# Four single rows in attention, low weight bits by GpSimd, the first feed-forward tiles turned by VectorE and DMA, in a new order

## The chip, the cores and the metric

One core of a Trainium2 chip. Times are microseconds (us) of that core. The kernel before took 346.61 us (median of 3 runs, 345.60 to 346.94).

## What is computed

Chunked attention with memory keys, and a feed-forward layer with SoLU and a normalization, all in float32:

```python
B, H, S, D = 4, 8, 768, 64            # chunk 32, left 16, right 8, 8 memory keys
for c in range(S // 32):               # each chunk of 32 queries sees 64 keys
    k_full, v_full = concat(mem, context of c)
    a = softmax(q_c @ k_full.T / 8)
    x[:, :, chunk c] = a @ v_full
x = x.transpose(0, 2, 1, 3).reshape(3072, 512)
h = x @ w_in                           # 512 x 1024
solu = h * softmax(h)
ln = (solu - mean) / sqrt(var + 1e-6) * g_ln
out = ln @ w_out                       # 1024 x 512
```

The two large products are made from rounded parts: each operand is split into a high part and a low rest, and three products (high x high, high x low, low x high) are summed in PSUM. The weights come as float64 and are put together from the two 32-bit words of each number.

## The kernel before

The 3072 tokens are 24 row tiles of 128. Attention works by items: rows 0 and 1 are an item each (`SINGLES = 2`), the other 22 rows go in 11 pairs. The feed-forward layer works row by row. `ORDER` (L31) is a list of steps that is read once from front to back (L600); a step issues its instructions, so the list sets the order of every engine's queue and of the queue of transfers on SyncE. There is no planner at run time: an engine takes its own instructions in this order and waits where an operand or a buffer isn't there yet.

The steps, with their engines:

- **Loads** (SyncE): `Lq`, `Lk`, `Lv` an item's queries, keys and values (L224); `D` 1 MB of weight words (L255; 0 to 3 are `w_in`, 4 to 7 `w_out`).
- **Weights**: `A` (ScalarE, L259) makes a float32 from the high word, `B` (VectorE, L267) shifts it left by 3, `I` (VectorE, L271) inserts the three top bits of the low word, `H` (L277) rounds to the high part, `L` (L285) makes the low rest. Weight block 0 goes in two cuts.
- **Attention**: `S` scores on TensorE (L343), `M` row maximum, `Bm` difference from it, `Z` sum with its reciprocal (VectorE, L366 to L414), `X` exponentials (ScalarE), then the probabilities are turned: items 0 to 3 by TensorE (`PT`, L332) and a copy `PC`; the others by VectorE in 32x32 blocks (`Pt`, L300) and four transfers of 128 KB (`Pw`, L309) that put the blocks in their place. `V` values on TensorE (L421), `N` division by the sum (VectorE, L446). The result x is turned likewise (`XT` for items 0 to 3, `Xt` and `Xw` for the others) and split (`XH`, `XL`).
- **Feed-forward**: `Gt.c.half` (L500) is three 128x512 matmuls of row t; eight of them make a row of h, in a two-bank PSUM buffer ("two", of which there are 3, shared with scores, values and turned tiles of pairs). `Hm`, `He`, `Hu` are maximum, exponential, product; `C` centers, `Sq` squares, `Dn` the inverse deviation. Then u is turned: rows 0 to 3 by TensorE (`UT`), the others by VectorE and transfers (`Ut`, `Uw`). `UH`, `UL` split it (L485, L492), and `Ot.f` (L567) is three matmuls with `w_out`, eight to a row. `Os`, `St` scale and store.
- `Wu5` (L201) is five matmuls of a zero tile, ten instructions, without use for the result.

Turning by TensorE and turning by VectorE with transfers leave the columns of a tile in different orders. The columns of `w_in` are sorted on the host for the second way; a row that is turned by TensorE reads `w_in` through a rearranged view instead:

```python
        if f"UT{t}" in todo:
            w = [m.rearrange("p (f d n) -> p f n d", d=4, n=SQ) for m in w]
```

Of the kernel before, what the change touches and what calls it, by code (L numbers as in the profile page):

```python
# [13 lines left out]
U32 = mybir.dt.uint32  # L14
AF = mybir.ActivationFunctionType
# [3 lines left out]
P = 128  # L19
# [3 lines left out]
SLOTS, HALVES, RAWS, ROUNDED = 7, 6, 4, 8  # L23
SINGLES = 2
AHEAD = 6
SPLIT = {0: 2}
# [9 lines left out]
Lk3 G1.0.1 H2.0@S L2.0@V G0.2.0 G1.1.0 N2 A4.0 B4.0 I4.0 A6.0 B6.0 L2.1@G G0.2.1 G0.3.0 G0.3.1 Hm0  # L36
G1.1.1 I6.0 XT2 XH2@S XL2@V He0 Lg H4.0@S H4.1@S L4.1@G G1.2.0 G1.2.1 G1.3.0 Hu0 G1.3.1 Hm1 He1 S3
M3 Bm3 G3.0.0 G3.0.1 G3.1.0 G3.1.1 D5 D7 G3.2.0 G2.0.0 G3.2.1 Hu1 G3.3.0 G3.3.1 A5.0 B5.0 X3 PT3
C0@S I5.0 G2.0.1 G2.1.0 C1@G A7.0 Lv3 PC3@S V3 G2.1.1 G2.2.0 G2.2.1 L4.0@G Hm3 He3 Z3 Lv5 Hu3 C3@S
UT3 UH3@S N3 XT3 B7.0 XH3@S I7.0 G2.3.0 G2.3.1 UL3@V O3.0 Lk4 H5.0@S Lq4 S4 XL3@V G4.0.0 G4.0.1 O3.1  # L40
G4.1.0 G4.1.1 H6.0@S Hm2 He2 Lq5 M4 Bm4 UT0 Lv4 Sq3 G4.2.0 Hu2 Lk6 X4 Pt4 H5.1@S Lk5 S5 G4.2.1 UH0@S
UL0@V O0.0 M5 Bm5 G5.0.0 L5.1@V L5.0@G O3.2 Lq7 X5 G5.0.1 UT1 UH1@S O0.1 Pw4 Pt5 G5.1.0 Pr4 H6.1@S
Sq0 H7.0@S Dn3@G L6.0@G O0.2 Dn0@G UL1@V G5.1.1 O0.3 G5.2.0 Z4 L7.0@G V4 N4 Xt4 G4.3.0 O3.3 G4.3.1
Hm4 Lq6 S6 Pw5 O0.4 He4 Lk7 Xw4 O3.4 G5.2.1 H7.1@S L6.1@G O0.5 G5.3.0 M6 Bm6 S7 Hu4 O0.6 O3.5 L7.1@V
O0.7 Os0 Pr5 V5 O3.6 C2@G Xr4 XH4@G XL4@G O1.0 M7 Bm7 X7 Lk8 G5.3.1 Z5 N5 X6 O3.7 Lv7 G7.0.0 G6.0.0
Lq8 Xt5 G7.0.1 G6.0.1 St0 Xw5 G7.1.0 O1.1 Os3 G7.1.1 G6.1.0 G7.2.0 Z6 Sq1 G6.1.1 G7.2.1 Lv6 Pt6 O1.2
G7.3.0 Hm5 He5 Hu5 C5@G Ut5 Pw6 UT2 O1.3 G6.2.0 Xr5 XH5@G O1.4 G7.3.1 UH2@S UL2@V O2.0 Hm7 O1.5 He7
# [43 lines left out]
def chunked_attention_then_solu_kernel(  # L91
# [132 lines left out]
    def load(name, src):  # L224
        def step(i):
# [463 lines left out]
```

## Time and profile before

| | |
|---|---|
| median of 3 runs | 346.61 us |
| the profiled execution | 345.05 us |
| its span (first to last instruction) | 343.3 us |
| mean granted TensorE clock | 0.985 |
| TensorE busy | 324.0 us, 94% of the span |
| VectorE busy | 223.3 us, 65% |
| GpSimd busy | 139.7 us, 41% |
| ScalarE busy | 130.2 us, 38% |
| moved by DMA | 62.38 MB, mean 182 GB/s |

The span is the profiled execution without 1.75 us that lie around it. PE is TensorE, DVE VectorE, ACT ScalarE, POOL GpSimd, SP SyncE. L513 is the line of the hidden layer's matmuls, L573 that of the second product, L353 scores, L437 values, L339 turning on TensorE, L204 the matmuls of zeros. Matmuls overlap, so the time of one is read from a run of them (start to start), not from the mean duration of one. "Issue" is time in which an engine waited for nothing that the profile shows.

### The profile page before, as it was taken

To read this page: it belongs to the slowest core of one execution; us is meant where nothing else is said; L and a number is where in the kernel's file an instruction comes from. 1 tells how busy PE (TensorE), PEld (TensorE's weight loads), DVE (VectorE), ACT (ScalarE), POOL (GpSimd) and SP (SyncE) were. 2 spreads that over 40 slices of the span, in tenths; PEclk is the share of its full clock that TensorE was granted. 3 is DMA by queue.
4 is the path that set the end of the run, shared out by engine and by line. 5 is a ranking of instruction groups with operands and counts; after the bars stand their busy time and mean duration, and the time that the engine had idled before them with its cause. 6 is when DMAs were issued, how large, how long until landed. Compare 5 with 4: busy or idle time off the path is not lost.

```text
span 343.3 us, 9936 instructions
## 1 busy us (share of the span) xinstructions
PE 324.0 (94%) x4324; PEld 262.4 (76%) x4324; DVE 223.3 (65%) x286; ACT 130.2 (38%) x189; POOL 139.7 (41%) x173
## 2 busy tenths in 40 slices
PE   1769999999889999999999999999999999999995
PEld 1657777887678888878888888888888888888784
DVE  1699998987993898866985764737467563046200
ACT  3257364743322243403432315422345175033421
POOL 0228052416216375455525702521176645525250
PEclk9969999999989999999999999999999999999999
DMA  7999933645839276775838686824342505144421
GB/s 292 418 423 414 413 146 109 228 138 164 313 86 329 65 185 153 216 225 151 321 76 251 164 272 138 277 67 113 105 123 64 122 2 122 61 126 133 110 94 61
DMA packets 32299, 62.38 MB, mean 182 GB/s; under 512 B 3712, under 2 KB 23168, under 8 KB 29824
## 3 DMA queue, kind: packets, MB, share of 16 engines
q1 hardware_dynamic: 28800, 55.46, 51.5%
q10 hardware_dynamic: 3456, 6.29, 5.0%
q8 instruction: 34, 0.56, 0.6%
q14 instruction: 9, 0.07, 0.1%
HBM read 35.52 MB, written 6.29 MB: 122 GB/s over the span
## 4 chain that ended last, share of the span: by engine, by line
PE 94%; issue 2%; DMA 2%; DVE 1%; ACT 0%; SPq 0%
PE two L513 40%; PE one L573 39%; PE two L353 6%; PE two L437 5%; PE two L339 2%; DMA k<-in_kw 2%; PE two L204 1%; PE one L339 1%; DVE half L454 0%; DVE half L387 0%; DVE per_head L376 0%; ACT half L581 0%; ACT half L400 0%; SPq L233 0%; SPq L257 0%
## 5 line engine op out<-in xcount | busy, mean ns | idle before, releaser
L513 PE MATMUL two<-w_in_h,fr 128*128 128x512 f32 x384 | 141.3, 401 | 0.0
L573 PE MATMUL one<-w_out_h,fr 128*128 128x512 f32 x384 | 137.9, 396 | 0.0
L513 PEld LDWEIGHTS two<-w_in_h,fr 128*128 128x128 f32 x384 | 72.3, 188 | 18.1
L573 PEld LDWEIGHTS one<-w_out_h,fr 128*128 128x128 f32 x384 | 72.6, 189 | 16.2 <-ACT half L581 0.3
L513 PE MATMUL two<-w_in_l,fr 128*128 128x512 f32 x192 | 76.3, 397 | 0.0
L573 PE MATMUL one<-w_out_l,fr 128*128 128x512 f32 x192 | 75.3, 392 | 0.0
L522 DVE TENSOR_REDUCE per_row<-two 128x1 f32<-128x1024 f32 x24 | 29.1, 1213 | 28.7 <-PE two L513 28.7
L581 ACT ACTIVATE half<-one,per_row 128x512 f32<-128x512 f32 x24 | 16.5, 687 | 81.5 <-PE one L573 73.9
L513 PEld LDWEIGHTS two<-w_in_l,fr 128*128 128x128 f32 x192 | 36.1, 188 | 8.1
L573 PEld LDWEIGHTS one<-w_out_l,fr 128*128 128x128 f32 x192 | 36.3, 189 | 7.2
L220 POOL TENSOR_TENSOR fr<-raw,fr 128x1024 fp32r<-128x1024 f32 x13 | 31.4, 2417 | 16.9 <-ACT fr L215 16.2
L527 ACT ACTIVATE raw<-two,per_row 128x1024 f32<-128x1024 f32 x15 | 16.8, 1118 | 35.1 <-DVE per_row L522 31.0
L353 PE MATMUL two<-k,q 64*32 64x64 f32 x1536 | 20.3, 236 | 10.0 <-DMA k<-in_kw 7.6
L353 PEld LDWEIGHTS two<-k,q 64*32 64x32 f32 x1536 | 17.4, 110 | 14.6 <-DMA q<-in_qT 7.6
L537 DVE CUSTOM_DVE_ANT_0 raw<-two,raw 128x1024 f32<-128x1024 f32 x15 | 18.3, 1218 | 10.9 <-ACT raw L527 9.5
L220 POOL TENSOR_TENSOR fr<-slot,fr 128x1024 fp32r<-128x1024 f32 x9 | 21.6, 2405 | 7.7 <-ACT fr L215 3.6
L217 POOL TENSOR_SCALAR fr<-slot 128x1024 fp32r<-128x1024 f32 x10 | 10.5, 1054 | 34.1 <-PE one L573 22.2
L562 POOL TENSOR_SCALAR per_row<-per_row,per_row 128x1 f32<-128x1 f32 x24 | 7.0, 292 | 39.7 <-ACT raw L554 29.9
L554 ACT ACTIVATE raw<-raw 128x1024 f32<-128x1024 f32 x15 | 15.7, 1049 | 9.0 <-DVE slot L305 9.0
L376 DVE TENSOR_REDUCE per_head<-two 128x16 f32<-128x1024 f32 (+1 forms) x13 | 14.8, 1140 | 5.0 <-PE two L353 4.7
L305 DVE STREAM_TRANSPOSE slot<-raw 128x1024 f32<-128x1024 f32 x12 | 14.8, 1237 | 4.1 <-ACT raw L547 2.6
L549 POOL TENSOR_SCALAR raw<-raw,per_row 128x1024 f32<-128x1024 f32 x6 | 6.8, 1126 | 26.2 <-DVE per_row L540 26.2
(92 smaller groups left out, 375.8 us busy)
## 6 DMA issues: line engine op xcount, KB each, us to landing
v<-in_vw SPq DMA_DIRECT2D x11, 1024.0 KB, 5.8
k<-in_kw SPq DMA_DIRECT2D x11, 672.0 KB, 7.5
slot<-raw SPq DMA_DIRECT2D x48, 128.0 KB, 2.8
out<-half ACTq DMA_DIRECT2D x24, 256.0 KB, 3.2
q<-in_qT SPq DMA_DIRECT2D x11, 512.0 KB, 4.6
raw<-slot SPq DMA_DIRECT2D x44, 128.0 KB, 2.6
raw<-in_w_in SPq DMA_DIRECT2D x4, 1024.0 KB, 9.0
raw<-in_w_out SPq DMA_DIRECT2D x4, 1024.0 KB, 9.1
```

The costliest lines, as they stand in the source:

```text
L220: (nc.gpsimd if on == "G" else nc.vector).tensor_tensor(out, a, b, ALU.subtract)
L305: nc.vector.transpose(t, src.rearrange("p (m d n) -> p d m n", d=4, n=SQ))
L353: nc.tensor.matmul(s[32 * j:32 * j + 32, r, t, g], q[rows, o + t, g, 32 * j:32 * j + 32], k[rows, o + t, g, START[j]:START[j] + KEYS], sta ...
L376: nc.vector.tensor_reduce(nmax, s, axis=AX.X, op=ALU.max, negate=True)
L437: nc.tensor.matmul(x[32 * j:32 * j + 32, r, t, g], pT[rows, t, g, j], vv[rows, o + t, g, j], start=True, stop=True,)
L513: nc.tensor.matmul(h[:, half], x[a], w[b], start=c == 0 and i == 0, stop=c == NC_ - 1 and i == 2,)
L522: nc.vector.tensor_reduce(take("per_row", ("hm", t), 1), flat(get("h", t)), axis=AX.X, op=ALU.max, negate=True)
L527: nc.scalar.activation(take("slot", ("u", t), 2), flat(get("h", t)), AF.Exp, bias=get("hm", t), scale=1.0, accum_out=take("per_row", ("esu ...
L537: nc.vector.tensor_tensor_reduce(u, flat(get("h", t)), u, 1.0, 0.0, ALU.mult, ALU.add, accum_out=usum)
L554: nc.scalar.activation(u, u, AF.Square, accum_out=take("per_row", ("var", t), 1))
L573: nc.tensor.matmul(get("o", t), u[a], w[b][:, f], start=f == 0 and i == 0, stop=f == NF - 1 and i == 2)
L581: nc.scalar.mul(take("half", ("osb", t), 1), get("o", t), get("rstd", t))
```

## The change

- `SINGLES = 4`: rows 0 to 3 are items of their own; 10 pairs follow.
- Step `B` is gone. A new step `T` makes the three low bits: GpSimd reads the top byte of the low word as uint8 (every eighth byte), and computes (byte - 15.5) / 32, which is rounded to an integer as it is written; `I` now shifts and inserts in one instruction.
- No `UT` is left: rows 0 to 3 of u go by `Ut` and `Uw` like the others, and their `G` steps read `w_in` straight. `XT` and `PT` stay for items 0 to 4 (rows 0 to 5, as before), and `N` of these items writes pairs of columns, with `vw` sorted to match on the host.
- The reciprocal is a step of its own, `Zr`: for 10 of 14 items on GpSimd, as a power of -1.
- In rows 0 to 3, `G` is two of the three products, and `K` is the third (high x low), so that it can come later. `G`, `K` and `O` steps come in any order of c and f; the first one to run starts the sum.
- Transfers of turned tiles may be issued by ScalarE (`@S`, 11 of them) instead of SyncE (`@Y`).
- Small pools: 7 instead of 6 "half" buffers, fewer of the smallest.
- The list is new from end to end: `Wu24`, `Wu9` and `Wu1` in place of two `Wu5`, and another order of loads.

```diff
-SLOTS, HALVES, RAWS, ROUNDED = 7, 6, 4, 8
-SINGLES = 2
+SLOTS, HALVES, RAWS, ROUNDED = 7, 7, 4, 8
+SINGLES, AHEAD, AHEAD_X = 4, 6, 6
+SPLIT, SPLIT_ROWS = {0: 2}, 4
 ORDER = """
-D0 CT A0.0 B0.0 A0.1 Lq0 B0.1 I0.0 H0.0@S Lk0 S0 M0 Lq2 Lk2 Bm0 Lk1 Lq1 X0 I0.1 H0.1@S L0.0@G Wu5 Z0
-L0.1@G S2 M2 D3 A3.0 Lv0 D1 PT0 Lv1 D2 Lv2 S1 M1 Bm2 Bm1 X1 PT1 PC0@S B3.0 I3.0 V0 H3.0@G L3.0@G
-H3.1@S Wu5 D4 Z1 D6 A1.0 PC1@S X2 N0 XT0 V1 B1.0 I1.0 H1.0@G L1.0@G PT2 N1 XT1 XH0@S H1.1@S Lq3
-XL0@V G0.0.0 G0.0.1 G0.1.0 A2.0 PC2@S V2 B2.0 XH1@S I2.0 H2.1@S L1.1@G XL1@V G1.0.0 L3.1@G G0.1.1 Z2
...
+Lq1 CT Wu24 D0 T0.0@G A0.1 A0.0 T0.1@G Lk1 Lk3 S1 D3 I0.0 H0.0@G Lq0 T3.0@G I0.1 M1 Bm1 X1 Z1 PT1
+H0.1@G Lq2 Lq3 A3.0 I3.0 H3.1@S H3.0@G S3 Lk2 M3 Bm3 X3 S2 M2 Bm2 Wu9 L0.0@G Zr1@G L0.1@V Lk0 S0 D2
+T2.0@G Z3 A2.0 M0 Bm0 X2 Z2 PT2 PC2@S Lv2 I2.0 D1 T1.0@G PC1@S Zr2@G X0 Z0 V2 PT0 Lv0 A1.0 PT3 PC0@S
+V0 I1.0 H1.0@S Zr0@V N0 Lv1 V1 N1 PC3@S L1.0@V Wu1 H2.1@S XT0 XH0@S XL0@V H1.1@S XT1 Lk4 XH1@S
+K0.1.0 N2 Lv3 V3 H2.0@S L3.0@G D7 K0.0.0 A7.0 G0.0.0 Lq4 L3.1@G G0.2.0 K0.3.0 XL1@V G1.2.1 G0.1.1
...
-    def w_first(i, x):
-        a = cut(get("a", i).bitcast(U32), i, x)
-        nc.vector.tensor_scalar(a, a, 3, None, ALU.logical_shift_left)
+    def low_byte(i, x):
+        w = get("raw", i).bitcast(U8).rearrange("p (n b) -> p n b", b=8)
+        n = w.shape[1] // SPLIT.get(i, 1)
+        return w[:, x * n:(x + 1) * n, 3]
+    def w_bits(i, x, on):
+        t = words(i, x, 0)
+        byte = low_byte(i, x)
+        if on == "S":
+            nc.scalar.activation(t, byte, AF.Identity, bias=down, scale=1.0 / 32)
+        else:
+            nc.gpsimd.tensor_scalar(t, byte, -15.5, 1.0 / 32, ALU.add, ALU.mult)
     def w_insert(i, x):
         a = cut(get("a", i).bitcast(U32), i, x)
-        low = cut(words(i, 0), i, x)
-        nc.vector.scalar_tensor_tensor(a, low, 29, a, ALU.logical_shift_right, ALU.bitwise_or)
+        nc.vector.scalar_tensor_tensor(a, a, 3, words(i, x, 0), ALU.logical_shift_left, ALU.bitwise_or)
...
     def row_sum(i):
...
-        nc.vector.tensor_scalar(s, s, 1e-9, None, ALU.add)
-        nc.vector.reciprocal(s, s)
+    def inverse(i, on):
+        s = get("rinv", i)[:, 0:2 * items[i][1] * NP_]
+        if on == "G":
+            nc.gpsimd.tensor_scalar(s, s, 1e-9, 1.0, ALU.add, ALU.mult)
+            nc.gpsimd.tensor_tensor(s, s, minus[:, 0:s.shape[1]], ALU.pow)
+        else:
+            nc.vector.tensor_scalar(s, s, 1e-9, None, ALU.add)
+            nc.vector.reciprocal(s, s)
...
     def norm(i):
         if f"XT{i}" in todo:
-            x = x.rearrange("p (n m r a) -> p r n a m", m=SQ, r=2, a=2)
+            x = x.rearrange("p (n m r a) -> p r n m a", m=SQ, r=2, a=2)
             for r in range(2):
                 nc.vector.tensor_tensor(
-                    x[:, r], xp[:, r].rearrange("p n (a m) -> p n a m", a=2),
-                    rinv[:, r].unsqueeze(3).broadcast_to([P, n * NP_, 2, SQ]), ALU.mult,
+                    x[:, r], xp[:, r].rearrange("p n (m a) -> p n m a", a=2),
+                    rinv[:, r].unsqueeze(3).broadcast_to([P, n * NP_, SQ, 2]), ALU.mult,
...
+    HH, HL, LH = ("xh", "h"), ("xh", "l"), ("xl", "h")
+    def hidden(products):
+        def step(t, c, half):
+            mine = products if t < SPLIT_ROWS else (HH, HL, LH)
+            for x, w in mine:
...
+                nc.tensor.matmul(h[:, half], xx, ww, start=n == 1, stop=n == 3 * NC_)
...
-                nc.sync.dma_start(t[:, e * q:e * q + e], src[SQ * q:SQ * q + SQ])
+                (nc.scalar if on == "S" else nc.sync).dma_start(
+                    t[:, e * q:e * q + e], src[SQ * q:SQ * q + SQ]
+                )
```

## Rows read from the trace of the kernel before

**Rows 1.** Page of the profile: its first line, and part 1, busy time by engine

```profile
span 343.3 us, 9936 instructions
...
PE 324.0 (94%) x4324; PEld 262.4 (76%) x4324; DVE 223.3 (65%) x286; ACT 130.2 (38%) x189; POOL 139.7 (41%) x173
```

**Rows 2.** Waits of TensorE: engine, line, waited-for, us in total, times, longest

```profile
PE two L353 <- DMA k<-in_kw: 7.6, 1, 7.6
...
PE two L353 <- issue: 2.3, 1, 2.3
PE two L437 <- issue: 2.2, 1, 2.2
```

**Rows 3.** Chain that ended last, in order of time: start, us, what; hidden-layer matmuls

```profile
53.13 1.63 PE two L513 x6
...
140.31 5.44 PE two L513 x24
```

**Rows 4.** Five-microsecond windows, columns: us, PE, PEld, DVE, ACT, POOL, PEclk, DMA share, GB/s

```profile
20.00:25.00 5.00, 4.43 (x85) 3.77 (x86) 4.78 (x9) 4.10 (x6) 1.91 (x2) 0.62 1.01 419
25.00:30.00 5.00, 4.79 (x86) 3.55 (x85) 4.81 (x6) 3.65 (x5) 4.10 (x4) 1.00 1.01 416
...
50.00:55.00 5.00, 5.00 (x56) 3.52 (x55) 4.12 (x5) 2.50 (x3) 3.32 (x3) 1.00 0.00 0
```

**Rows 5.** The same chain: one row tile turned on TensorE, and what follows

```profile
67.93 0.87 PE two L339 x8
68.80 0.70 PE two L513 x3
```

**Rows 6.** The same chain: scores of a pair of row tiles, and what follows

```profile
62.87 1.41 PE two L353 x91
64.28 1.58 PE two L513 x6
```

**Rows 7.** The same chain: the gap inside the values of item 5, and the last piece

```profile
93.15 2.23 issue
95.39 1.07 PE two L437 x54
96.45 2.73 PE one L573 x6
...
339.67 0.69 ACT half L581
```

**Rows 8.** Timeline of the start: start, us, engine, line, operation

```profile
8.72 2.50 PE L204 MATMUL two<-z 128*128 128x128 f32 x10
...
24.50 1.23 DVE L274 SCALAR_TENSOR_TENSOR slot<-raw,slot 128x1024 uint32<-128x1024 uint32 x1
...
27.48 0.52 PE L513 MATMUL two<-w_in_h,fr 128*128 128x512 f32 x1
...
28.39 2.17 DVE L274 SCALAR_TENSOR_TENSOR slot<-raw,slot 128x1024 uint32<-128x1024 uint32 x1
```

**Rows 9.** Groups by line and form: busy us, mean ns, idle before

```profile
L269 DVE TENSOR_SCALAR slot<-slot 128x1024 uint32<-128x1024 uint32 x5 | 3.6, 725 | 0.0
...
L376 DVE TENSOR_REDUCE per_head<-two 128x8 f32<-128x512 f32 x2 | 1.4, 692 | 3.0 <-PE two L353 3.0
...
L387 DVE TENSOR_TENSOR half<-two,per_head 128x512 f32<-128x512 f32 x2 | 1.4, 686 | 0.0
...
L454 DVE TENSOR_TENSOR half<-two,per_head 128x256 f32<-128x256 f32 x4 | 2.2, 648 | 0.2 <-PE two L437 0.2
...
L217 POOL TENSOR_SCALAR fr<-slot 128x1024 fp32r<-128x1024 f32 x10 | 10.5, 1054 | 34.1 <-PE one L573 22.2 <-DMA slot<-raw 10.5 <-DMA slot<-slot 1.3
...
L563 POOL TENSOR_TENSOR per_row<-per_row,mhalf 128x1 f32<-128x1 f32 x24 | 13.3, 553 | 2.0
```

**Rows 10.** The same groups: a transpose on VectorE, and a weight rest on VectorE

```profile
L305 DVE STREAM_TRANSPOSE slot<-raw 128x1024 f32<-128x1024 f32 x12 | 14.8, 1237 | 4.1 <-ACT raw L547 2.6 <-POOL raw L549 1.3
...
L220 DVE TENSOR_TENSOR w_in_l<-slot,w_in_h 128x512 fp32r<-128x512 f32 x1 | 0.6, 627 | 0.0
```

More of the change, by code (lines that the diff above doesn't have):

```diff
@@ L87 @@
+St20 O23.5 O23.6 Dn23@G O23.1 O23.2 Os23 St23
 """
@@ L377, in row_max @@
         used("s", i)
-    todo = set(ORDER.split())
+    todo = set(ORDER.replace("@", " ").split())
     def below_max(i):
@@ L398, in exps @@
     def exps(i):
-        a = get("p", i)
-        nc.scalar.activation(a, a, AF.Exp, scale=scale)
+        if f"Bm{i}" in todo:
+            a = get("p", i)
+            nc.scalar.activation(a, a, AF.Exp, scale=scale)
+            return
+        n = items[i][1] * NP_
+        nmax = get("nmax", i)[:, 0:2 * n]
+        nc.scalar.mul(nmax, nmax, scale)
+        a = take(home(i), ("p", i), 2).rearrange("p (n r k) -> p r n k", r=2, k=KEYS)
+        for r in range(2):
+            for h in range(n):
+                nc.scalar.activation(
+                    a[:, r, h], by_head(i)[:, r, h], AF.Exp, bias=nmax[:, r * n + h:r * n + h + 1], scale=scale
+                )
+        used("s", i)
+        used("nmax", i)
     def row_sum(i):
@@ L468, in source, with target @@
         return (name + "t", i), get(name + "t", i).rearrange("p (q m n) -> p m q n", q=4, n=SQ)
-    def target(name, i, uses):
+    def target(name, i):
         if name[0] == "u":
-            return by_block(take("fr", (name, i), uses))
+            return by_block(take("fr", (name, i), NF))
         first, n = items[i]
-        buf = shared("fr", (name, first // 2), uses)
+        u = first // 2
+        each = [2 if t < SPLIT_ROWS and name == "xh" else 1 for t in (2 * u, 2 * u + 1)]
+        buf = shared("fr", (name, u), 2 * NC_ * sum(each))
         o = first % 2 * HALF
@@ L498, in low @@
         return step
[L500 to L519 removed]
+    HH, HL, LH = ("xh", "h"), ("xh", "l"), ("xl", "h")
+    def hidden(products):
+        def step(t, c, half):
+            u, odd = divmod(t, 2)
+            mine = products if t < SPLIT_ROWS else (HH, HL, LH)
+            h = shared("two", ("h", t), 2)
+            for x, w in mine:
+                xx = get(x, u).rearrange("p (t c n) -> p t c n", t=2, n=P)[:, odd, c]
+                ww = (w_in_h if w == "h" else w_in_l)[:, c, half * HALF:(half + 1) * HALF]
+                if f"UT{t}" in todo:
+                    ww = ww.rearrange("p (f d n) -> p f n d", d=4, n=SQ)
+                n = done[t, half] = done.get((t, half), 0) + 1
+                nc.tensor.matmul(h[:, half], xx, ww, start=n == 1, stop=n == 3 * NC_)
+            for x in sorted({x for x, _ in mine}):
+                used(x, u)
+        return step
     def h_max(t):
@@ L567, in project @@
     def project(t, f):
-        if f == 0:
-            take("one", ("o", t), 1)
+        o = shared("one", ("o", t), 1)
         u = [get(n, t)[:, f * P:(f + 1) * P] for n in ("uh", "ul")]
         w = (w_out_h, w_out_l)
-        for i, (a, b) in enumerate(((0, 0), (0, 1), (1, 0))):
-            nc.tensor.matmul(
-                get("o", t), u[a], w[b][:, f], start=f == 0 and i == 0, stop=f == NF - 1 and i == 2
-            )
-        if f == NF - 1:
-            used("uh", t)
-            used("ul", t)
+        for a, b in ((0, 0), (0, 1), (1, 0)):
+            n = done[t] = done.get(t, 0) + 1
+            nc.tensor.matmul(o, u[a], w[b][:, f], start=n == 1, stop=n == 3 * NF)
+        used("uh", t)
+        used("ul", t)
     def scale_out(t):
```

208 lines of the change are left out of this document (92 added, 116 removed).

## The prediction

> **What bounds the kernel now.** I read the page first: TensorE is busy for 324.0 of 343.3 us, the next engine, VectorE, for 223.3 [rows 1]. Then the waits of TensorE: what costs more than a fraction of a microsecond is the wait for the first keys (7.6), one for the probabilities of row 1, and two of about 2.2 us, called issue, which no buffer or operand explains [rows 2]. The third view is the chain that ended last. From the first hidden-layer matmul, which starts at 27.48 us [rows 8], to the last scaling at 339.67 [rows 7] it is TensorE's own work nearly throughout. So there are two prices: what comes off TensorE's work in these 312 us comes off the time, one for one, as long as the other engines keep up; and ahead of 27.48 us a chain of transfers, VectorE and ScalarE decides.
>
> The reader should look at two things within the 312 us. A hidden-layer step has three matmuls. In the stretch at 140.31, 24 of them take 5.44 us: 0.2267 each. But at 53.13 six take 1.63: 0.272 each [rows 3]. The granted clock is 1.00 there, and the transfers are at rest from 50 to 55 us [rows 4], so it is neither. What sets this stretch apart is the row: it belongs to rows 0 to 3, which read `w_in` through the rearranged view of `UT`.
>
> **Part by part, on TensorE.**
> Turning of u for rows 0 to 3: four times eight transposes, 0.87 us each, and the step behind takes 0.70 instead of 0.68 [rows 5]. It goes to VectorE and transfers: 4 x 0.89 = -3.6 us.
> Straight reading of `w_in`: four rows of 24 matmuls, 96 x (0.272 - 0.2267) = -4.4 us. The Trainium skill (TensorE: Matmul & The Clock Gate, Wait — 56ns, not 53.3ns?) has the distance of matmuls at full clock set by their columns alone. By that this term would be nothing and the sum 4.4 us higher; here the two kinds differ by 20% at the same clock, and the measurement decides.
> Scores and values: a pair takes 1.41 us and about 0.22 more in the step behind it (1.58 for six matmuls that take 1.36) [rows 6]. Before, values of one pair that is now single rows are computed behind 27.48, after it those of row 3 alone: half of 1.41, -0.7. The transposes of x and of the probabilities are as many as before, and so are the matmuls: splitting a step into `G` and `K` adds none.
> The gap at 93: values of item 5 stop halfway for 2.23 us; the two steps that then run as six matmuls take 2.73 instead of 1.36, and the second half of the values takes 1.07 where half of 1.41 would do [rows 7]. That is 2.23 + 1.37 + 0.36, about -4.0 if it doesn't come back. It came while scores and values of pairs ran close together: nine matmuls, 2 us, lie between scores 7 and values 5 in the old list. In the new one no two steps of scores or values of pairs have fewer than 15 between them, 3.4 us. I therefore take it as gone; the other bound is that one such gap comes elsewhere, 0, and two would be +4.
>
> **The start.** The first keys come behind the same bytes as before (a 1 MB block and one row's queries), so at 7.6 us [rows 2]. `Wu24` is 48 instructions. The first ten of before took 2.50 us [rows 8], a turned tile takes 0.109 per instruction when the engine is fast [rows 5]: between 5.2 and 11.7 us. TensorE began to work at 7.6, and all ten of those, from 8.72 to 11.2, were slow; so I take 3.6 us at that rate, 15 at 0.24 and 33 at 0.14, over at about 9.3; scores of row 1 end at 10. Then VectorE has an unbroken list up to x of rows 0 and 1: four maxima, four differences and four sums at 0.69 [rows 9], three inserts at 1.23 [rows 8], one rest of 0.63 [rows 10], two divisions of at most 2 x 0.65 [rows 9], 0.6 of small ones: 8.3 + 3.7 + 0.6 + 2.6 + 0.6 = 15.8. With `L1.0` (0.63) and half a microsecond of waits the first `K` runs at 26.9, -0.6 against 27.48. The bounds: 4 earlier (the zeros end before the keys come, the divisions are shorter with paired columns) and 4 later (zeros at the slow rate to the end, or an issue gap as the one of 2.3 us in the scores before [rows 2]).
> The nine shifts `B` (0.73 for a whole block [rows 9]) go. On the path that is three of them, which the list above no longer has; the others are nothing, as VectorE has free time later. Nine `T` come on GpSimd; the nearest row is a one-operand pass of 1.05 us [rows 9]. `T1.0` is the last on the path and runs beside `A1.0`: nothing, and about 1 us if it comes behind it. The reading of every eighth byte may raise it, at most to the two-fold, in the same place.
> **Clock.** TensorE has waits ahead of the first step in either list, and the granted clock fell to 0.62 between 20 and 25 us [rows 4]. Before, ten useless matmuls ran in that stretch and the clock was full from 25 on; now two do (`Wu1`). Half a clock over the first 2 to 3 us: +1.0 (0 to +3).
>
> **What the others must now do.** Four times a transpose of 1.24 on VectorE [rows 10] against the subtractions `UL` of these rows that move from VectorE to GpSimd: about even, and the shifts and reciprocals that leave it make it lighter. The four transfers of each of the four rows, and their issue on SyncE, lie under the hidden steps of rows 1 to 4, some 25 us of TensorE's work from the end of row 0 to its first use; what is queued behind `Uw0` on SyncE is the queries and values of item 6, which are wanted only behind the values of item 5. 44 issues on ScalarE's queue lie in its free 62%. New waits in a list of which every place has changed: I take +1.5, with 0 below (there is hardly one now) and +6 above (three or four rows of h that wait for a buffer held by VectorE).
>
> **Sum.** -3.6 - 4.4 - 0.7 - 4.0 - 0.6 + 1.0 + 1.5 = -10.8. The profiled execution took 345.05 (1.75 around its span), which gives 334.2. The median of the runs shown is 1.56 above it: 335.8, say 336.
>
> **The rivals.**
> *The gap comes back.* Nothing in the trace names its cause, only its neighbourhood; instructions of scores and values are still issued by the hundred, and transfers move 419 GB/s ahead of the first step [rows 4]. Then 340.
> *VectorE and GpSimd in each other's way.* An insert beside GpSimd's subtractions took 2.17 us, one of the same form alone 1.23 [rows 8]. GpSimd gets the nine `T`, the `UL` of four rows and the reciprocals, most of it in the first 60 us, where VectorE is the second busiest. Eight such collisions behind the start and on the path would add 8 x 0.9 = 7: 343. Against it: TensorE has a stock of steps that can run, and hardly waited for VectorE so far. The Trainium skill (GPSIMD Engine Reference, Engine selection) would keep such elementwise passes on VectorE, and says (Key points) that the two share interfaces to the memory; the two inserts agree.
> *Slower: the power on GpSimd.* A power of one column takes 0.55 us [rows 9]. If its price went by columns, a reciprocal of 8 would take 4.4 and one of 16 8.8. `Zr1`, `Zr2` and `Zr4` stand in GpSimd's queue ahead of the rests `L3`, `L1`, `L2` and of `L4`, and the hidden steps of rows 0 and 1 need those: 2 x 4.4 ahead of `L3.0` and 8.8 ahead of item 4's division, 17.6 in all, as TensorE then runs dry. 345 - 12.3 + 17.6, and the median's 1.6, is 352. It turns at 12.3 us for 32 columns, 0.38 us a column. Against it: one column in 0.55 is little more than the other one-column operations of GpSimd in the profile.
> *The slow matmuls aren't due to the view.* Then 4.4 stay, 340 (what the rule named above would give). The stretch with idle transfers speaks against it.
>
> **How the numbers follow.** Forecast as summed 0.50; gap again 0.20; collisions 0.13; the power 0.06; matmuls not faster 0.04; 0.07 for a wait that I don't see. The range takes in the gap, the slow matmuls and most of the collisions: up to 343; below, a start 4 us earlier and no new waits: 336 - 5 = 331. 0.5% is 1.7 us, about what a measurement of this kernel tells from no change. Faster than 344.9: 0.50 + 0.20 + 0.04 + most of the 0.13 and some of the rest, 0.88. Slower than 348.3: the power and a part of the unseen, 0.08. Between: 0.04.
>
> **What would show it.** Right: six hidden matmuls in 1.36 from the first row on; no transposes of u on TensorE; the first hidden matmul at 25 to 28 us; GpSimd's power at 1 us or less; no issue gap behind 30 us; TensorE's work unbroken to the end. Wrong: a wait of TensorE for VectorE or GpSimd of several microseconds in the first 60 us, or rows 0 to 3 still at 0.272.

## The result, and the profile after

Over 20 runs each, the changed kernel takes 349.12 us (median) and the kernel before 346.10: the ratio is 1.0073, with a 95% interval of 1.0051 to 1.0096. The change makes the kernel slower by 0.7%; 336.0 had been forecast. The profiled execution of the changed kernel took 346.47 us, 1.42 more than the one of before, and the readings of this section are of that one. It is the second fastest of the 20 (345.68 to 355.00), 2.65 below their median, so it shows 1.4 of the 3.0 us between the medians; what the rest may be comes with the traces of later runs. Every ratio here leaves out disturbed executions, and the profiled ones of two later runs (zeros narrow, four loads later) were such, with longer spans (351.0 and 355.4 us), so that from these two only single waits ahead of 80 us are read.

The head of the page, the busy time of each engine, and from the part on queues the one by which instructions come:

```profile
span 344.7 us, 10028 instructions
...
PE 323.9 (94%) x4340; PEld 265.2 (77%) x4340; DVE 212.7 (62%) x271; ACT 136.1 (39%) x196; POOL 169.5 (49%) x199
...
q8 instruction: 34, 0.56, 0.7%
```

TensorE is as busy as before [rows 1], with fewer transposes, more useless matmuls, and more of its time at half clock (mean granted clock 0.979 instead of 0.985). What it waited for (engine, line, waited-for, us in total, times, longest):

```profile
PE two L359 <- issue: 4.0, 1, 4.0
PE two L463 <- issue: 3.9, 2, 2.3
PE one L598 <- ACT half L603: 3.9, 2, 3.0
PE one L345 <- ACT half L407: 2.6, 2, 2.3
```

The wait for the first keys [rows 2] is gone from the list, because 48 useless matmuls now fill it. Instead of 4.5 us there are 7.9 called issue, in three places, and 3.9 for ScalarE's scaling of the second product. The three places are in TensorE's timeline of the start (start, us, engine, line, operation, in brackets the idle time before):

```profile
1.04 7.97 PE L212 MATMUL two<-z 128*128 128x128 f32 x48 [1.04 <-DVE z L199]
8.94 0.86 PE L359 MATMUL two<-k,q 64*32 64x64 f32 x64
...
12.62 1.65 PE L359 MATMUL two<-k,q 64*32 64x64 f32 x105
18.22 0.65 PE L359 MATMUL two<-k,q 64*32 64x64 f32 x23 [3.96 <-issue]
18.80 4.21 PE L212 MATMUL two<-z 128*128 128x128 f32 x18
...
27.81 0.99 PE L463 MATMUL two<-v,half 64*32 64x64 f32 x74 [0.46 <-ACT half L223]
31.09 0.77 PE L463 MATMUL two<-v,half 64*32 64x64 f32 x54 [2.30 <-issue]
...
33.41 0.49 PE L541 MATMUL two<-w_in_l,fr 128*128 128x512 f32 x1
33.83 0.84 PE L463 MATMUL two<-v,half 64*32 64x64 f32 x62
36.32 0.30 PE L463 MATMUL two<-v,half 64*32 64x64 f32 x2 [1.65 <-issue]
36.55 0.67 PE L541 MATMUL two<-w_in_l,fr 128*128 128x512 f32 x1
```

One hidden step runs alone at 33.41; the steady run begins at 36.55. Before it began at 27.48 [rows 8], and 26.9 was forecast. So the start is 9.1 us longer. From there to the last matmul of the second product the kernel before took 312.2 us [rows 7, 8]; now it is from 36.55 to 340.9, 304.35, which is 7.8 less. 9.1 - 7.8 and 0.1 at the tail are the 1.4 us of the profiled executions.

The 7.8 can be seen directly. In rows 0 to 3 six hidden matmuls took 1.63 us [rows 3]; the same timeline has now, at 67 us:

```profile
67.29 0.39 PE L541 MATMUL two<-w_in_l,fr 128*128 128x512 f32 x1
67.52 1.29 PE L541 MATMUL two<-w_in_h,fr 128*128 128x512 f32 x5
68.65 0.39 PE L541 MATMUL two<-w_in_l,fr 128*128 128x512 f32 x1
```

From 67.29 to 68.65 are six matmuls: 1.36. No u is turned on TensorE any more, and in this execution there is no stop in the values of item 5:

```profile
70.56 1.48 PE L463 MATMUL two<-v,raw 64*32 64x64 f32 x128
```

Against that stand two things. Windows of five microseconds (us, then busy time and count of PE, PEld, DVE, ACT, POOL, then granted clock, DMA share, GB/s):

```profile
15.00:20.00 5.00, 1.78 (x28) 1.61 (x28) 1.65 (x3) 1.77 (x2) 4.20 (x4) 0.50 1.01 411
...
25.00:30.00 5.00, 2.94 (x146) 2.38 (x146) 4.86 (x9) 3.69 (x7) 3.70 (x3) 1.00 1.02 416
...
35.00:40.00 5.00, 3.68 (x10) 2.82 (x11) 3.96 (x7) 0.89 (x1) 4.67 (x5) 0.67 0.87 351
```

Behind the first stop and the last the granted clock is at its lower level: 0.50 from 15 to 20 us, where TensorE had stood for 3.96, and 0.67 on the mean from 35 to 40, where the steady run begins; its first ten matmuls take 3.96 us (36.55 to 40.51) instead of 2.27. And the wait for ScalarE, 2.97 us of it before 112.95, is seen in the timelines of ScalarE (and its queue, ACTq) and of GpSimd:

```profile
103.62 6.15 ACTq L329 DMA_DIRECT2D raw<-raw  x4
...
108.54 1.22 ACTq L329 DMA_DIRECT2D raw<-raw  x2
...
112.21 0.69 ACT L603 ACTIVATE half<-one,per_row 128x512 f32<-128x512 f32 x1 [0.16 <-POOL per_row L588]
```
```profile
107.60 2.91 POOL L437 TENSOR_TENSOR per_head<-per_head,minus 128x16 f32<-128x16 f32 x1
```

Four issues of a move hold ScalarE's queue for 6.15 us. (The row at 108.54 is from a view of that window alone and shows the last two of the four.) The issues themselves are short, 0.55 to 0.58 each; between the second and the third the queue waits 3.7 us, until 108.54. The trace shows what for: the third issue waits on a semaphore that a load of v from SyncE's queue uses too, and that load landed at 108.52. ScalarE's computation stands behind it. And GpSimd's power for item 6 stands ahead of the root of the row (`Dn`) that the scaling needs; in this execution the root, over at 112.18, is what came last. The price of that power, by form:

```profile
L437 POOL TENSOR_TENSOR per_head<-per_head,minus 128x16 f32<-128x16 f32 x8 | 23.3, 2909 | 0.7
L437 POOL TENSOR_TENSOR per_head<-per_head,minus 128x8 f32<-128x8 f32 x2 | 3.3, 1666 | 0.2
```

### The profile page after: what moved, and what is told of

It reads as the page before. It is cut to its first block, busy times and chain, and to the rows that moved or that the text cites. A ratio compares the mean times of both kernels' runs of the same rounds, so it can differ in the third digit from the quotient of the medians.

```text
span 344.7 us, 10028 instructions
## 1 busy us (share of the span) xinstructions
PE 323.9 (94%) x4340; PEld 265.2 (77%) x4340; DVE 212.7 (62%) x271; ACT 136.1 (39%) x196; POOL 169.5 (49%) x199
## 4 chain that ended last, share of the span: by engine, by line
PE 71%; DVE 9%; issue 4%; DMA 4%; POOL 4%; SPq 4%; ACT 2%; ACTq 0%; POOLq 0%
PE one L598 32%; PE two L541 27%; PE two L463 4%; PE two L212 4%; PE two L359 4%; SPq L329 4%; POOL per_head L437 3%; DMA v<-in_vw 2%; DVE per_row L547 2%; DMA slot<-slot 1%; DVE per_head L382 1%; DVE slot L318 1%; DMA slot<-raw 1%; ACT half L603 1%; DVE slot L574 1%
## 5 line engine op out<-in xcount | busy, mean ns | idle before, releaser
L598 PE MATMUL one<-w_out_h,fr 128*128 128x512 f32 x384 | 131.2, 393 | 3.9 <-ACT half L603 3.9
L541 PE MATMUL two<-w_in_h,fr 128*128 128x512 f32 x384 | 130.8, 398 | 0.0
L225 POOL TENSOR_SCALAR fr<-slot 128x1024 fp32r<-128x1024 f32 x15 | 15.8, 1050 | 42.9 <-PE two L541 18.8
L228 POOL TENSOR_TENSOR fr<-slot,fr 128x1024 fp32r<-128x1024 f32 x12 | 29.6, 2470 | 14.6 <-DMA raw<-slot 10.0
L437 POOL TENSOR_TENSOR per_head<-per_head,minus 128x16 f32<-128x16 f32 (+1 forms) x10 | 26.6, 2660 | 0.8
L228 DVE TENSOR_TENSOR fr<-slot,fr 128x1024 fp32r<-128x1024 f32 x10 | 12.8, 1282 | 21.3 <-POOL fr L225 21.3
L552 ACT ACTIVATE slot<-two,per_row 128x1024 f32<-128x1024 f32 x12 | 13.4, 1115 | 30.6 <-DVE per_row L547 27.6
L228 POOL TENSOR_TENSOR fr<-raw,fr 128x1024 fp32r<-128x1024 f32 x7 | 16.8, 2393 | 14.0 <-ACT fr L223 13.5
L552 ACT ACTIVATE raw<-two,per_row 128x1024 f32<-128x1024 f32 x12 | 13.4, 1113 | 23.8 <-DVE per_row L547 21.4
L562 DVE CUSTOM_DVE_ANT_0 raw<-two,raw 128x1024 f32<-128x1024 f32 x12 | 14.6, 1216 | 12.0 <-ACT raw L552 11.9
L562 DVE CUSTOM_DVE_ANT_0 slot<-two,slot 128x1024 f32<-128x1024 f32 x12 | 14.6, 1220 | 9.2 <-ACT slot L552 9.2
```

Source lines behind the costliest of these rows:

```text
L225: nc.gpsimd.tensor_scalar(out, in_, 1.0, 0.0, ALU.mult, ALU.add)
L228: (nc.gpsimd if on == "G" else nc.vector).tensor_tensor(out, a, b, ALU.subtract)
L437: nc.gpsimd.tensor_tensor(s, s, minus[:, 0:s.shape[1]], ALU.pow)
L541: nc.tensor.matmul(h[:, half], xx, ww, start=n == 1, stop=n == 3 * NC_)
L552: nc.scalar.activation(take("slot", ("u", t), 2), flat(get("h", t)), AF.Exp, bias=get("hm", t), scale=1.0, accum_out=take("per_row", ("esu ...
L562: nc.vector.tensor_tensor_reduce(u, flat(get("h", t)), u, 1.0, 0.0, ALU.mult, ALU.add, accum_out=usum)
```

## The experiments

**What the stops have in common.** Every wait of TensorE called issue, of 0.3 us and more, was counted by its place in TensorE's stream, that is by the recorded instructions of TensorE (weight loads, matmuls, and the few waits for semaphores between them) that lie ahead of it. The places come out on one grid; six of the fourteen traces:

```
kernel                        place: us of the stop
before                        449: 2.29   3521: 2.23
changed                       449: 3.96    961: 2.29   1217: 1.65
first run (zeros wide)        449: 1.71    705: 2.18    961: 3.59   1729: 2.09   3009: 0.59
moves by SyncE                961: 2.44   1217: 2.00   2497: 2.60
reciprocals on VectorE        961: 2.49   1217: 1.27   1473: 1.98   2497: 3.12
rows 2 and 3 later            449: 1.20   1729: 1.40   3009: 0.31
```

All are 449 plus a multiple of 256, and so are all those of the other eight traces but one, which is told below (the turning alone, first try). The instruction queue moves 34 packets of 16384 bytes in the changed kernel (0.56 MB). Ahead of the steady run its packets begin at 15.7, 22.2, 28.8 and 34.0 us of the span, one every five to seven microseconds, and where TensorE had stopped it goes on 2.3 to 2.5 us after a packet's start (2.2 to 2.7 in all traces). In the start the packets follow TensorE: while the loads run at about 415 GB/s, one begins 2.9 to 4.0 us after TensorE passes a place of the grid (6.3 for the first), and at 43.8, with the transfers down to 32 GB/s from 40 to 45 us, 0.8 us after. The theory that the runs test: TensorE's instructions arrive in blocks of 256; scores or values of two single rows, or of a pair, use up a block in 1.4 to 1.7 us (0.86 for one row above, 1.41 for a pair [rows 6]), and while the loads fill the transfer engines the next block comes only 5 to 7 us after. The Trainium skill (Runtime: NRT & Kernel Launch, Instruction fetch mechanics) has blocks of 16 KiB, 256 instructions, which the sequencer fetches over a queue of its own, with the cost mostly hidden behind issue. The size and the queue agree with the packets here; that it is hidden does not, by the 7.9 us above.

**Zeros wide.** The useless matmuls of `Wu24` and `Wu9` do four times the columns in a quarter of the instructions; 100 instructions fewer come ahead of the first hidden step.

```diff
-        for _ in range(n):
-            nc.tensor.matmul(z_ps, z, z, start=True, stop=True)
+        m = 4 if n >= 4 else 1
+        for _ in range(n // m):
+            nc.tensor.matmul(z_ps.rearrange("p (m c) -> p m c", m=m), z,
+                z.unsqueeze(1).broadcast_to([P, m, P]), start=True, stop=True)
```

> Theory of blocks: TensorE's instructions come in blocks of about 255, each by a transfer of its own that is slow while the other transfers run at full rate; the changed list runs 1080 of them ahead of its first hidden step, the old one 856. Here the useless matmuls take the same time with a quarter of the instructions (100 fewer). The first gap, now behind the 41st matmul of the third group of scores (about 442 instructions), moves about 100 instructions on, into the scores of row 0, the next ones likewise; the steady run of hidden matmuls starts at 31 to 33 us instead of 36.5, and the time falls by 3 to 5 us. Theory of the zeros' time: it is the 4.2 us of useless matmuls at half clock ahead of the scores of row 0 that delay the start; they stay, so start and time stay within 1 us.

Measured: 348.88 us, ratio 1.0063 (1.0032 to 1.0094). The first stop moved from the scores of row 2 to nine matmuls into the scores of row 0, as a count of instructions asks. But the time did not follow: further stops came at 705 and 961, in V1 for 3.59 us, and the steady run began at 35.28, where 31 to 33 had been expected. A hundred instructions are less than a block.

**Zeros narrow.** As many instructions, each of 16 columns.

```diff
-            nc.tensor.matmul(z_ps, z, z, start=True, stop=True)
+            nc.tensor.matmul(z_ps[:, 0:16], z, z[:, 0:16], start=True, stop=True)
```

> The counterpart: as many useless matmuls as in the changed kernel, each of 16 columns instead of 128, so nearly no time and the same number of instructions. Blocks: the gaps stay at the same counts of instructions (behind the 41st matmul of the third group of scores, in the values of row 1, in those of row 3), and the steady run of hidden matmuls starts at 33 us or later. Zeros' time: the scores of row 0 run 4 to 5 us earlier, there is no gap ahead of them, and the steady run starts at 32 us or before.

Measured: 350.20 us, ratio 1.0048 (1.0005 to 1.0091). The stop stayed at the place 449, and 18 zeros still took 4.02 us (granted clock 1.00), where 18 of 128 columns had taken 4.21 (granted clock 0.50). So this edit did not take the zeros' time away, and it does not test the theory of the zeros' time; the run without zeros below does. Both runs leave the place of a stop to the count.

**The turning alone, first try.** The kernel before, with u of rows 0 to 3 turned by VectorE and transfers right behind its centring.

```diff
-C0@S I5.0 G2.0.1 G2.1.0 C1@G A7.0 Lv3
+C0@S Ut0 Uw0 I5.0 G2.0.1 G2.1.0 C1@G Ut1 Uw1 A7.0 Lv3
...
-C3@S UT3 UH3@S
+C3@S Ut3 Uw3 UH3@S
```

> The kernel before with one part of the change alone: u of rows 0 to 3 turned by VectorE and transfers, so that these rows read w_in straight. The prediction's two terms, 3.6 and 4.4: hidden matmuls of rows 0 to 3 at 0.227 us apart, 32 transposes fewer, about 8 us less, ratio 0.972 to 0.985 with up to 3 us of new waits. Rival (the other engines then set the pace and the gain is given back as waits): ratio over 0.993.

Measured: 355.66 us, ratio 1.0246 (1.0203 to 1.0288). SyncE's own queue in the timeline, and what TensorE lost:

```profile
51.70 2.58 SPq L327 DMA_DIRECT2D slot<-raw  x4
54.39 2.50 SPq L327 DMA_DIRECT2D raw<-raw  x4
56.98 1.04 SPq L240 DMA_DIRECT2D v<-in_vw  x2
```
```profile
62.24 2.04 PE L444 MATMUL two<-v,raw 64*32 64x64 f32 x128 [8.67 <-issue]
```

The moves wait for u, and the load of v behind them was issued at 56.98, so the values wait for it from 53.57 until 62.24. The profile calls this wait issue too, but it lies on no grid: the load is what is late. So the part is not free on TensorE where a load is queued behind its moves.

**Moves by SyncE.** The changed kernel, with the moves of ScalarE's queue given to SyncE's; and **reciprocals on VectorE**, the changed kernel without GpSimd's power.

```diff
-Pw7@S Xw6@S Uw5@S Uw6@S Uw8@S Xw9@S Pw12@S Xw11@S Uw10@S Uw16@S Uw23@S
+Pw7@Y Xw6@Y Uw5@Y Uw6@Y Uw8@Y Xw9@Y Pw12@Y Xw11@Y Uw10@Y Uw16@Y Uw23@Y
```
```diff
-Zr1@G Zr2@G Zr4@G Zr5@G Zr6@G Zr7@G Zr8@G Zr9@G Zr12@G Zr10@G
+Zr1@V Zr2@V Zr4@V Zr5@V Zr6@V Zr7@V Zr8@V Zr9@V Zr12@V Zr10@V
```

> The changed kernel with all transfers of turned tiles issued by SyncE. Theory: ScalarE, held up while it issues transfers, is late with the scaling of rows of the result, and TensorE waits 3.9 us for it; these waits go, 2 to 4 us less. Rival: SyncE's queue then makes tiles late, and nothing is won or up to 3 us lost.

> The changed kernel with all reciprocals on VectorE, as before (0.74 + 0.25 us for an item there, against 0.2 + 2.9 on GpSimd). Theory of the power: GpSimd's 26.6 us of powers stand ahead of inverse deviations and rests, part of TensorE's waits for the scaling of rows; 1 to 3 us less. Theory that the start alone has lost the gain: within 1 us of the changed kernel, and the steady run of hidden matmuls starts at 35 us or later as there.

Measured: 348.02, ratio 1.0020 (0.998 to 1.0061), and 349.89, ratio 1.0114 (1.0061 to 1.0168). TensorE's wait for ScalarE's scaling fell from 3.9 to 1.8 us and to 0.9, and the time did not fall with it: the stops on the grid are 7.0 and 8.9 us in these two (table above). Alone neither edit pays. Both kernels run the changed kernel's steps on TensorE and have its stops in V1 and V3 (961 and 1217), 4.4 and 3.8 us together; their steady runs begin at 34.69 and 34.15, as the stop at 449 is missing. And both have a stop that the profiled execution of the changed kernel did not have, in the values of item 5 at the place 2497; the first one's:

```profile
73.51 0.31 PE L468 MATMUL two<-v,raw 64*32 64x64 f32 x7 [2.60 <-issue]
```

The other two kernels with the same steps in the same order on TensorE (zeros narrow, four loads later) have it too, 4.11 and 3.54 us.

**Rows 2 and 3 later.** Wide zeros, and the values of rows 2 and 3 and the scores of item 4 moved behind the first hidden steps: 850 instructions come ahead of the first of these, where the changed kernel has 1080.

```diff
-Z0 V2 PT0 Lv0 A1.0 PT3 PC0@S V0 ... K0.1.0 N2 Lv3 V3 H2.0@S ... Lv4 S4 G1.2.0 ... M4 Bm4 Lk6 A4.0
+Z0 PT0 Lv0 A1.0 PT3 PC0@S V0 ... K0.1.0 Lv3 H2.0@S ... G0.1.1 V2 N2 ... K1.1.1 V3 Zr3@V N3 G1.2.0
+... G0.3.0 S4 M4 Bm4 Lk6 Lq7 ... K1.3.1 X4 PT4 G1.0.1
```

> The changed kernel with the wide zeros, and the values of rows 2 and 3 and the scores of item 4 moved behind the first hidden steps: 850 instead of 1080 instructions of TensorE ahead of the first hidden step. Theory of blocks: gaps again only at multiples of 256 from the 449th on; two of them (449, 705) lie ahead of the first hidden step, not three and a half; the steady run starts at 27 to 30 us, and the time falls by 5 to 8 us against the changed kernel, ratio to the kernel before 0.985 to 0.995. Rival (weights and VectorE set the start, and blocks only fill time that was lost anyway): the run starts at 32 us or later, less than 2 us won.

Measured: 347.25 us, ratio 1.0005 (0.9971 to 1.0038). In its timeline and its windows:

```profile
18.41 0.78 PE L368 MATMUL two<-k,q 64*32 64x64 f32 x55 [1.20 <-issue]
...
28.62 0.70 PE L550 MATMUL two<-w_in_l,fr 128*128 128x512 f32 x2 [0.94 <-ACT fr L232]
```
```profile
40.00:50.00 10.00, 6.76 (x154) 5.14 (x153) 8.01 (x10) 6.18 (x9) 3.64 (x3) 1.00 0.90 338
```

The steady run begins at 28.62, 7.9 us earlier, with one stop of 1.20 ahead of it. That is in the theory's range, but some 1.7 of the 7.9 are only moved: the values of rows 2 and 3, 0.86 us each, now stand behind the start. Only some 2 us reach the end, where 5 to 8 had been expected: 3.2 are lost between 40 and 50 us, 1.8 of them to the exponentials of item 4, which now come too late, and the copy behind them, 1.4 to the stop at 1729; and TensorE waits 4.3 us for ScalarE's scaling.

**All together.** The same, with the moves on SyncE and the reciprocals on VectorE.

> e6 with all reciprocals on VectorE and all transfers of turned tiles issued by SyncE. If start, power and ScalarE's queue are separate losses, 337 to 341 us, ratio 0.975 to 0.985, TensorE without a wait for ScalarE behind 45 us. If GpSimd and ScalarE had free time to lose, no more than 1 us below e6.

Measured: 342.16 us, ratio 0.9872 (0.9829 to 0.9915), the first that beats the kernel before, though above the 337 to 341 expected. TensorE waits for no scaling any more, and no stop on the grid is over 0.6 us. With the stops gone, VectorE is next in the start: TensorE waits 1.78 us for its division of row 1 and begins the hidden steps at 30.30. The largest loss after that is between 40 and 50 us:

```profile
46.03 1.09 PE L354 MATMUL two<-ident,slot 128*128 128x128 f32 x8 [1.38 <-ACT slot L416]
```

**No zeros at all.** The same without `Wu`, which takes 36 instructions away (18 matmuls and their weight loads).

> e7 without any useless matmul, 36 instructions fewer. Blocks: the gaps stay at the same counts, so they move 36 instructions on in the work; start within 1 us of e7. Clock: TensorE does its first scores and the first hidden steps at half clock; if that decides, the steady run starts 2 to 4 us later than in e7.

Measured: 343.05 us, ratio 0.9906 (0.9874 to 0.9938), which is not told apart from the run before. The useless matmuls are worth no more than about a microsecond either way: without them TensorE waits 7.2 us for the first keys and stops 3.38 us at the place 449, and the hidden steps begin at 30.12 instead of 30.30. So the time of the zeros is not what delays the start.

**Four loads later.** The changed kernel, with the loads for item 4 and two blocks of `w_out` given to ScalarE's queue behind `XH1`.

```diff
-XT1 Lk4 XH1@S K0.1.0 N2 Lv3 V3 H2.0@S L3.0@G D7 K0.0.0 A7.0 G0.0.0 Lq4 ... N3 D4
+XT1 XH1@S Lk4@S Lq4@S D7@S D4@S K0.1.0 N2 Lv3 V3 H2.0@S L3.0@G K0.0.0 G0.0.0
...
-T7.0@G
+A7.0 T7.0@G
```

> The changed kernel, with four loads that nothing wants before 40 us (k and q of item 4, two blocks of w_out) issued by ScalarE behind the high part of x of row 1, at about 33 us, instead of by SyncE at 18 to 22 us. Theory (TensorE's instructions come in blocks of 256 over a queue of their own, and a block comes more slowly while the 16 engines are full): the transfers fall off between 22 and 33 us, and the two gaps of the changed kernel at the instructions 961 and 1217 (2.30 and 1.65 us) shrink to under 1.0 together; the steady hidden run starts at 32 to 34 instead of 36.55. Rival (a block takes its time whatever the other transfers do, or the gaps belong to the values): the gaps stay within 0.5 us of 3.95 together and the run starts at 36 or later. The whole time is no clean measure, since what these loads bring is late for item 4 and the second blocks of w_out: -3 to +4 us against the changed kernel.

Measured: 354.72 us, ratio 1.0149 (1.007 to 1.0228); TensorE waits 4.27 us for the queries of item 4, from 35 us on. What the run was made for is its start. Its windows and its timeline:

```profile
20.00:25.00 5.00, 3.56 (x151) 2.75 (x157) 3.90 (x7) 3.26 (x5) 2.73 (x3) 1.00 0.74 290
25.00:30.00 5.00, 3.72 (x171) 2.91 (x172) 4.86 (x10) 3.21 (x6) 4.15 (x4) 1.00 0.88 305
```
```profile
24.91 1.77 PE L468 MATMUL two<-v,half 64*32 64x64 f32 x128 [0.46 <-ACT half L228]
...
30.88 0.30 PE L468 MATMUL two<-v,half 64*32 64x64 f32 x2 [0.30 <-issue]
31.10 0.50 PE L546 MATMUL two<-w_in_l,fr 128*128 128x512 f32 x1
```

V1 runs through: the stop at 961 is gone, the one at 1217 is 0.30. The three runs with the same steps on TensorE and the loads in their old place have 3.9, 4.4 and 3.8 us there. The transfers between 20 and 30 us move about 300 GB/s instead of 415, and the packet behind the place 705 begins 1.1 us after TensorE passes it, where it took 3.4 to 3.7 in those three. The steady run begins at 31.10. Against 36.55 that is 5.5 us, but 2.4 of them are the first stop (1.53 instead of 3.96), which lies ahead of the moved loads; against the two kernels without that stop it is 3.1 to 3.6. So fuller transfers do slow the blocks, as far as one trace can show it, and the rival falls.

**Item 4 earlier, and item 4 later.** Two edits of the run with all together: its scores five hidden steps earlier, or its transposes and values three steps later.

```diff
-V3 Zr3@V N3 G1.2.0 ... G0.3.0 S4 M4 Bm4 Lk6 ... K1.3.1 X4 PT4 G1.0.1
+V3 Zr3@V N3 S4 G1.2.0 ... T7.0@G M4 Bm4 ... XL3@V X4 ... G1.1.0 PT4 A6.0 ... K1.3.1 G1.0.1
```
```diff
-X4 PT4 G1.0.1 K1.1.0 PC4@S V4 G1.1.1 He0 G1.0.0 Lv5 G1.3.1 G1.3.0
+X4 G1.0.1 K1.1.0 G1.1.1 PT4 G1.0.0 G1.3.1 PC4@S V4 He0 Lv5 G1.3.0
```

> As the run that puts all together (rows 2 and 3 later, moves on SyncE, reciprocals on VectorE: 342.16), but the scores of item 4, its maximum and its differences come some five hidden steps earlier and its transposes some eight steps later. There TensorE lost 2.1 us between 43 and 50 us to waits for the exponentials of item 4 and for what stands behind them. Theory: these are gone, nothing else moves: 340 us (339 to 342). Rival (VectorE, which has the second rows' divisions and rests in the same stretch, is late with these instead): 342 to 344, with TensorE waiting for XL1 or L2.1 between 33 and 43 us.

> The run that puts all together (342.16), with the transposes and the values of item 4 three hidden steps further back, so that TensorE, which waited there 1.38 us for the exponentials and 0.46 for the copy of the transposes, has steps of row 1 to run instead. Theory (these waits are order alone): 1.4 us off, 340.8 (340 to 342), TensorE's work between 40 and 50 us at 9 us instead of 7.9. Rival (the next row's hidden steps are late instead, for they want the buffer of row 0 that VectorE frees at 51 us): no change, 342, with a wait of TensorE of over 1 us for VectorE at about 51 us.

Measured: 345.04 us, ratio 0.9966 (0.994 to 0.9992), for the first; 341.90, ratio 0.9900 (0.9873 to 0.9927), for the second, in which the wait for the exponentials is 0.25 us. In turn a row of the first one's timeline, a window of it, and a row of the second one's timeline:

```profile
39.92 1.61 PE L368 MATMUL two<-k,q 64*32 64x64 f32 x95 [1.95 <-issue]
```
```profile
40.00:45.00 5.00, 5.00 (x108) 4.34 (x107) 3.31 (x4) 0.58 (x2) 0.00 (x0) 0.50 0.49 167
```
```profile
49.93 0.33 PE L472 MATMUL two<-v,slot 64*32 64x64 f32 x11 [1.46 <-issue]
```

In the first, neither theory nor rival: the scores, five steps nearer to the values of rows 2 and 3, ran out of instructions (place 1217), and TensorE, which had worked for 2.2 of the 5 us to 40, then ran 5 us at half clock. In the second the wait that was taken away came back as a stop in the values of item 4 (place 1729, 1.46 us), so nothing was won over 342.16, and the rival's wait for VectorE is not there either.

**The turning alone, second try.** The kernel before, with rows 0, 1 and 2 turned by VectorE, and their moves behind the loads.

```diff
-C0@S I5.0 G2.0.1 G2.1.0 C1@G A7.0 Lv3 ... Lq5 M4 Bm4 UT0 ... Lk5 S5 ... UT1 ... Ut5 Pw6 UT2
+C0@S Ut0 I5.0 G2.0.1 G2.1.0 C1@G Ut1 A7.0 Lv3 ... Lq5 Uw0 M4 Bm4 ... Lk5 Uw1 S5 ... Ut5 Uw2 Pw6
```

> The kernel before with one part of the change, placed so that no load stands behind it: u of rows 0, 1 and 2 is turned by VectorE and four transfers, issued behind the loads of item 5 and item 7, and these rows read w_in straight; row 3 stays on TensorE. By the terms of the prediction this takes 3 x 0.89 = 2.7 off TensorE's work for the transposes and 3 x 1.09 = 3.3 for the slow reading, -5.9 in all. Theory (these terms are real; in the earlier try only the loads that were held back ate them): 340 to 343, ratio 0.98 to 0.99. Rival (this part alone brings nothing, for VectorE or the transfers are full in the old list at this place): 345 or more.

Measured: 344.58 us, ratio 0.995 (0.9919 to 0.998). TensorE at the start, and two of its waits:

```profile
28.70 0.62 PE L520 MATMUL two<-w_in_h,fr 128*128 128x512 f32 x2
29.16 0.40 PE L520 MATMUL two<-w_in_l,fr 128*128 128x512 f32 x1
```
```profile
PE two L346 <- ACT slot L554: 1.3, 1, 1.3
PE one L580 <- ACT fr L222: 0.6, 1, 0.6
```

The steps run at 0.23 from the first, where before they took 0.27. But from the first of them (28.15 us) to the last matmul it is 310.0 us, 2.2 less than before, not 5.9: TensorE now waits 2.9 us for other engines and transfers (the two rows above, and three smaller), 2.7 on the grid where before it was 2.2, and the stop ahead of the start grew by 0.9. The terms are there; more than half of them is given back at once. That a list which was tight around TensorE's old speed has nothing ready when TensorE is faster is the likely reason, but it was not tested.

## Why the prediction was wrong

**The step that failed is "The start".** It counted what VectorE had to do ahead of the first hidden step, 15.8 us in one unbroken list from 10 us on, and bounded its issue gaps by the one of 2.3 us seen before. The list did begin at 9.83. But it was broken: VectorE in the changed kernel, in its timeline,

```profile
18.92 0.69 DVE L382 TENSOR_REDUCE per_head<-two 128x8 f32<-128x512 f32 x1 [3.31 <-PE two L359]
...
23.92 0.17 DVE L378 MEMSET two<- 32x128 f32 x1 [2.38 <-PE two L359]
...
31.91 0.76 DVE L480 TENSOR_TENSOR half<-two,per_head 128x256 f32<-128x256 f32 x2 [1.71 <-PE two L463]
```

waited 7.4 us for scores and values: 3.31 and 1.71 while TensorE had no instructions, and 2.38 while the zeros behind its first stop ran at half clock. The first hidden step came at 33.41, 6.5 us behind the 26.9 of the sum, and the steady run at 36.55. In the start it is TensorE's supply of instructions that binds: two runs moved it, one by fewer instructions ahead (28.62), one by emptier transfers (31.10), with VectorE's work ahead of the first hidden step unchanged in both. TensorE's stops ahead of the steady run are 7.9 us, before they were 2.3, and the values of two more rows cost 1.7; that is 7.3 of the 9.1 us, and the rest is not split here. The prediction's own sign, no issue gap behind 30 us, failed at 31.09 and 36.32. Singles for rows 2 and 3 bring the values of two more rows ahead of the first steady steps, and `Wu24` and `Wu9` are 132 recorded instructions, where the two `Wu5` of before were 40: 1080 weight loads and matmuls come ahead of the first hidden step instead of 856. The sum had a price for the time of `Wu24`, none for the 4.21 us of `Wu9`, and none for any of them as instructions.

**The terms on TensorE: right, but for the gap, which was luck.** Turning, reading and single values, and the gap in the values of item 5 taken as gone, were 12.7 us; 7.8 is the net from 36.55 on, after 3.9 for ScalarE and some 1.7 for the half clock at the start of the run. 7.8 + 3.9 + 1.7 is 13.4, within a microsecond. But the 4.0 us for the gap came true only in the profiled execution. In all four other traces with the same steps in the same order on TensorE, a stop of 2.60 to 4.11 us stands in the values of item 5 again, at the place 2497. In the profiled execution of the changed kernel the packet for that place began at 68.19, 3.5 us before TensorE came to it (71.72), and so nothing was lost. That such a stop is part of the 2.65 us between this execution and the median is likely, but not shown. The reason given for the gap's absence, that no scores and values of pairs come close together, does not hold: it is a matter of where in the stream 256 instructions run out, and how fast.

**Clock** (+1.0, to +3): 1.7 in the first ten matmuls. Right in size. **New waits** (+1.5, to +6): 3.9, within the bounds, but partly behind ScalarE's queue, which had been costed at nothing: the "44 issues in its free 62%" are short, but one of them waited 3.7 us for a load, and ScalarE's work stood behind it.

**The rivals.** The gap came back: in the start three times instead of once, and in four traces of five in the values of item 5 too; 340 had been worked out for one. The slower rival, the power on GpSimd, was not the cause: 8 columns take 1.67 and 16 take 2.9 us, 0.18 to 0.21 a column, half of the 0.38 at which it would have decided, and without it the kernel was no faster (349.89). But "1 us or less" was wrong too (one column in 0.55 was not little more than GpSimd's other one-column operations, which took 0.21 to 0.31 in the profile before), and in the last stretch ahead of 112 us it is one of two things that hold the scaling. VectorE and GpSimd in each other's way: not so, the inserts of a whole block took 1.22 to 1.53 us, and behind the start TensorE waited 0.2 us for VectorE. Slow matmuls: not so, 0.227 as soon as the clock is full, from row 0 on.

**Open.** The stop in the scores of row 2 was 3.96 us, 1.53, and none in two others, whose keys of row 2 came 1.0 us late instead, in four kernels with the same steps up to there. Their first packets began at 15.7, 13.4, 12.7 and 12.5 us; what sets that was not tried. Nor was a list made that puts steps with few instructions between all scores and values of the first 60 us: the best kernels here (341.90 and 342.16, which aren't told apart) still lose 2 us between 40 and 50.

## What to carry to other kernels

An idle time that the profile calls issue should be counted, not explained by its neighbours: if its places in the engine's stream lie 256 apart, the engine ran out of instructions, and what helped here was fewer instructions there, or fewer bytes moved at that time; off the grid it was a late load. This start was bound by three supplies, bytes, other engines and instructions, and work moved ahead of the first long steps has to be priced in all three. One trace is one execution: the stop that was missing in the changed kernel's stood in all four others with the same steps on TensorE. What a faster engine gives back shows only when the waits behind it are cleared in the same step: here reordering (347.25) and clearing (348.02, 349.89) each brought little or nothing, and all of it together 342.16.

## What the runs showed of the hardware that was not expected

- TensorE's stops called issue stand, but for one late load, at places 449 + 256k of its recorded instructions, and end 2.2 to 2.7 us after a 16384-byte packet of the instruction queue begins; beside loads at 415 GB/s these packets come 5 to 7 us apart ahead of the steady run, where scores or values use up 256 instructions in 1.4 to 1.7 us.
- A power of 16 columns on GpSimd takes 2.9 us and one of 8 takes 1.67, where one column takes 0.55 [rows 9].
- Eighteen matmuls of 16 columns took 4.02 us at a granted clock of 1.00, and eighteen of 128 columns 4.21 at 0.50.
- Four issues of a move held ScalarE for 6.15 us, though they take 0.55 to 0.58 each: one of them waited 3.7 us for a load from SyncE's queue with which it shares a semaphore, and ScalarE's computation waited behind it.
